# Dense MoE on one core: the first product by one level of Strassen's scheme, with its row operands kept in DRAM

## The chip, the core and the metric

One core of a Trainium2 chip. The metric is the device time of one execution in microseconds (us). The engines are named as in the profile: PE (TensorE, matmuls), PEld (its weight loads), DVE (VectorE), ACT (ScalarE), POOL (GpSimd), SP (SyncE, which issues most of the DMAs). Everything is float32; each matmul operand is split into a high and a low part, and each product is made of three matmuls, high·high, high·low and low·high.

## The reference

Three stages, each the input of the next (N = 2304 rows, D = 512, E = 8 experts, F = 1024):

```
# 1. attention with a threshold, 4 batches x 8 heads x 576 x 64
scores = scale * q @ k.T
scores = where(scores >= max(scores) - tau, scores, -1e9)
attn_out = softmax(scores) @ v            # -> x (2304, 512)

# 2. dense MoE: every row goes through every expert
P = exp(x @ w_gate - max)                 # then 8 rounds of row and column normalisation
for e in range(E):
    h = np.maximum(x @ w1[e], 0.0)        # (2304,512) @ (512,1024)
    out += P[:, e:e+1] * (h @ w2[e])      # (2304,1024) @ (1024,512)

# 3. top-1 MoE: each row goes through one expert, scaled by its gate
idx = argmax(x @ w_gate2); out[row] = gate * (relu(x[row] @ v1[idx]) @ v2[idx])
```

## The kernel before, in words

`attention` leaves x transposed (512 features on 4 x 128 partitions, 2304 rows along the free side) in the tile `xall`. `moe1` is the dense stage, `moe2` the top-1 stage. No queue is written by hand. Every piece of work is handed to a list planner (`Sched`) as `op(name, engine, cost, due time, function, what it depends on, acq, rel)`; `acq` and `rel` take and return counted resources such as PSUM banks ("h", "y") or buffers. The planner fills one list per engine, which is the order in which that engine then issues. An engine's list is strict: an instruction that waits holds up all behind it.

`moe1` before walks 8 experts; in each, 6 chunks of 384 rows; in each, 8 blocks of 128 columns of F. One block is

- `g1` (L567): 12 matmuls of 384 columns, x·w1 into one of 4 "h" banks,
- `relu_hi` on ACT (L572) and `relu_lo` on DVE (L576): the split of max(h, 0), 128x384,
- `g2` (L583): 3 row tiles x 3 matmuls of 512 columns into the chunk's 3 "y" banks.

At the end of a chunk DVE adds Pm[:, e] * y to the row sums `acc` (L691, `y_acc`), 128x512 each. Weights arrive by `ld_w` (L528, L530), are split by ACT (`rnd`, L539) and POOL (`w_lo`, L551). The rows of a chunk are split anew for each expert: `x_hi` on ACT (L539), `x_lo` on POOL (L560). `gate` (L598) forms the logits of the dense stage.

Before, `moe2` starts while the last expert of `moe1` runs: when a row tile's sum is final it is transposed (`tx1`, L872), split by ACT and DVE (`ev1` L881, `ev1l` L884), multiplied with the second gate (`lg1` L890, `lg3` L900), ranked, and stored. A table of row numbers then says which rows go to which expert. Row tiles below `TE` count into an early table, the others into a late one. Slots of gathered rows run through L1239 (first product, `hp`) and L1258 (second, `py`); their weights are loaded at L1195 and split at L1223 (ACT) and L1227 (DVE); the gathered rows are transposed at L1208 (`tx`) and split at L1216 and L1219.

Of the kernel before, what the change touches and what calls it, by code (L numbers as in the profile page):

```python
# [116 lines left out]
def attention(tc, sc, cst, dram, xT, q, k, v, tau, also=None):  # L117
# [11 lines left out]
    with ExitStack() as ctx:  # L129
# [296 lines left out]
        for p in range(NP):  # L426
# [70 lines left out]
            for half in range(2):  # L497
# [13 lines left out]

def moe1(tc, sc, cst, pools, xT, acc, wgs, w1, w2, NE=8, NW=9):
    nc = tc.nc
    E, Dm, FF = w1.shape
    N = xT[0].shape[1]
    CH = 384
    NCH, NF, NK, NT = N // CH, FF // 128, Dm // 128, N // 128
    one, wp, stg, xs_p, h_p, bank = pools
# [14 lines left out]
    WH = lambda e, f: V if e == 0 and f == 2 else A
    WL = lambda e, f: V if e == 0 and f != 2 else G
    XH = lambda e, c: A

    def rnd(eng, out, in_):
        if eng == A:
            nc.scalar.copy(out, in_)  # L539
        elif eng == V:  # L540
            nc.vector.tensor_copy(out, in_)
        else:
            nc.gpsimd.tensor_scalar(out, in_, 1.0, 1.0, op0=ALU.mult, op1=ALU.mult)

    def w_hi(e, f):
        wt[e, f] = wp.take()
        rnd(WH(e, f), wt[e, f][:, 0], wr[e, f])

    def w_lo(e, f):
        t = wt[e, f]  # L550
        (nc.vector if WL(e, f) == V else nc.gpsimd).tensor_tensor(t[:, 1], wr[e, f], t[:, 0].bitcast(F32), op=ALU.subtract)  # L551
# [936 lines left out]
```

## Time and profile before

| what | us |
|---|---|
| median of 3 runs (2291.84 to 2294.73) | 2293.86 |
| the profiled execution | 2292.15 |
| its span, first to last instruction | 2290.4 |
| attention | 0 to 338 |
| dense stage (`moe1`), its first and last `g1` | 342.9 to 1972.7 |
| top-1 stage, its main part | 1987 to 2235 |
| tail (last products, evictions, stores) | 2235 to 2290.4 |

The profile's page gives busy times over the whole span; a stage's limit is read from the windows (busy time of each engine in a stretch) and from the chain of waits (which work each step waited for, followed back from the last instruction). In the groups of instructions, "idle before" is the time in which the engine had nothing to do just ahead of such an instruction, and the releaser is what ended it.

### The profile page before, as it was taken

Reading aid. Unit: us, or ns where it says so; the run is one execution under the profiler, and the core shown is the slowest. Engines: PE = TensorE matmul, PEld = TensorE weight load, DVE = VectorE, ACT = ScalarE, POOL = GpSimd, SP = SyncE. Lnnn points to the kernel's source line nnn. Section 1 sums busy time; section 2 is a strip of 40 time slices with the busy share of each in tenths; the row PEclk is TensorE's granted clock in tenths of the full one; section 3 lists DMA queues with packets and bytes.
Section 4 is the critical chain, followed back from the end, with each engine's and each line's share of the span. In section 5 each row is a group of like instructions: output and inputs, shape, how many; then the busy total and the mean of one; then the engine's idle time right before and its main releaser. Section 6 shows DMA issues by size and latency. Waiting matters only on the chain.

```text
span 2290.4 us, 31977 instructions
## 1 busy us (share of the span) xinstructions
PE 2254.2 (98%) x12699; PEld 2048.7 (89%) x12699; DVE 887.6 (39%) x1904; ACT 780.0 (34%) x1394; POOL 634.5 (28%) x641
## 2 busy tenths in 40 slices
PE   7999999999999999999999999999999999999997
PEld 7999988888899999999999999999999888888886
DVE  8999973113412212211211212112112243775673
ACT  6888862113112211311221131122113121455673
POOL 6777762104302301410230141123014010021220
PEclk9999999999999999999999999999999999999999
DMA  3222112002000100200010020001001011568860
GB/s 95 64 59 63 43 44 83 1 1 74 1 1 19 56 1 1 74 1 1 19 56 1 1 74 1 1 19 56 1 1 37 14 28 33 218 226 298 277 213 13
DMA packets 101691, 129.66 MB, mean 57 GB/s; under 512 B 19006, under 2 KB 64206, under 8 KB 101520
## 3 DMA queue, kind: packets, MB, share of 16 engines
q1 hardware_dynamic: 97696, 118.10, 16.1%
q0 software_dynamic: 3840, 9.45, 1.1%
q8 instruction: 102, 1.67, 0.3%
q14 instruction: 53, 0.43, 0.1%
HBM read 118.52 MB, written 13.18 MB: 58 GB/s over the span
## 4 chain that ended last, share of the span: by engine, by line
PE 93%; issue 2%; DVE 2%; DMA 2%; ACT 1%; SPq 0%; POOL 0%; POOLq 0%; ACTq 0%; DVEq 0%
PE h L567 35%; PE y L583 35%; PE pt_av L407 4%; PE s L282 4%; PE py L1258 4%; PE hp L1239 4%; PE pt_m L350 2%; PE sh L1270 1%; PE pt_k L251 1%; PE sy L1300 1%; PE pt_av L410 1%; DMA out_dram<-ys,idi 0%; PE pt_q L241 0%; PE tx L1208 0%; PE lt L598 0%
## 5 line engine op out<-in xcount | busy, mean ns | idle before, releaser
L567 PE MATMUL h<-xs,w 128*128 128x384 f32 x4608 | 871.0, 337 | 1.6 <-ACT w L539 1.0
L583 PE MATMUL y<-w,hh 128*128 128x512 f32 x3456 | 867.0, 394 | 0.6 <-DVE hh L576 0.6
L567 PEld LDWEIGHTS h<-xs,w 128*128 128x128 f32 x4608 | 819.0, 188 | 35.7 <-ACT w L539 1.4
L583 PEld LDWEIGHTS y<-w,hh 128*128 128x128 f32 x3456 | 640.2, 188 | 117.9 <-DVE hh L576 1.0
L576 DVE SCALAR_TENSOR_TENSOR hh<-h,hh 128x384 fp32r<-128x384 f32 x384 | 214.1, 558 | 1210.4 <-ACT hh L572 1210.3
L572 ACT ACTIVATE hh<-h 128x384 fp32r<-128x384 f32 x384 | 188.9, 492 | 1173.5 <-PE h L567 1150.7
L560 POOL TENSOR_TENSOR xs<-xall,xs 128x384 fp32r<-128x384 f32 x192 | 189.1, 1017 | 1114.6 <-ACT xs L539 1114.6
L551 POOL TENSOR_TENSOR w<-wr,w 128x1024 fp32r<-128x1024 f32 x57 | 137.0, 2404 | 116.6 <-ACT w L539 112.3
L407 PE MATMUL pt_av<-PTh,vsp 128*128 128x288 f32 x512 | 144.4, 323 | 0.0
L1239 PE MATMUL hp<-xst,w 128*128 128x256 f32 x960 | 121.6, 284 | 0.2 <-DVE xst L1219 0.2
L1239 PEld LDWEIGHTS hp<-xst,w 128*128 128x128 f32 x960 | 117.7, 191 | 2.6 <-DVE xst L1219 1.6
L304 ACT ACTIVATE p<-s,stat 128x576 f32<-128x576 f32 x144 | 108.2, 753 | 29.8 <-DVE stat L287 29.5
L310 DVE SCALAR_TENSOR_TENSOR p<-s,stat,p 128x576 f32<-128x576 f32 x144 | 116.0, 808 | 5.0 <-ACT p L304 2.2
L1258 PE MATMUL py<-w,hp 128*128 128x512 f32 x480 | 113.1, 393 | 1.6 <-ACT hp L1246 0.9
L287 DVE TENSOR_REDUCE stat<-s 128x1 f32<-128x576 f32 x144 | 108.1, 752 | 12.7 <-PE s L282 12.4
L1258 PEld LDWEIGHTS py<-w,hp 128*128 128x128 f32 x480 | 88.9, 188 | 20.2 <-ACT hp L1246 1.2
L282 PE MATMUL s<-kk,qst 128*128 128x288 f32 x512 | 96.0, 310 | 2.5 <-DVE p L310 2.2
L539 ACT CAST w<-wr 128x1024 fp32r<-128x1024 f32 x63 | 66.1, 1049 | 92.1 <-PE y L583 85.6
L407 PEld LDWEIGHTS pt_av<-PTh,vsp 128*128 128x128 f32 x512 | 91.8, 188 | 1.5
L691 DVE SCALAR_TENSOR_TENSOR acc<-y,Pm,acc 128x512 f32<-128x512 f32 x126 | 86.5, 743 | 0.8 <-POOL acc L687 0.8
L539 ACT CAST xs<-xall 128x384 fp32r<-128x384 f32 x192 | 84.7, 511 | 0.0
L366 POOL TENSOR_TENSOR PTl<-rp,PTh 128x512 fp32r<-128x512 f32 x64 | 82.5, 1289 | 4.3
(237 smaller groups left out, 1780.3 us busy)
## 6 DMA issues: line engine op xcount, KB each, us to landing
wr<-in_moe_w_dram SPq DMA_DIRECT2D x128, 256.0 KB, 3.1
xall<-in_moe_w_dram SPq DMA_DIRECT2D x56, 512.0 KB, 5.3
acc<-in_moe_w_dram SPq DMA_DIRECT2D x56, 512.0 KB, 3.8
kr<-in_k_dram SPq DMA_DIRECT2D x16, 256.0 KB, 2.8
qr<-in_q_dram SPq DMA_DIRECT2D x16, 256.0 KB, 3.0
vr<-in_v_dram SPq DMA_DIRECT2D x16, 256.0 KB, 2.8
rbc<-rd SPq DMA_DIRECT2D x32, 128.0 KB, 3.0
x1d<-acc SPq DMA_DIRECT2D x28, 128.0 KB, 2.4
```

The lines of the kernel that those rows point to most:

```text
L282: nc.tensor.matmul(ps[:, half, 0:288], lh, kk[p][:, h, s, half * 288:(half + 1) * 288], start=(i == 0 and s == 0), stop=(i == len(parts) - ...
L310: nc.vector.scalar_tensor_tensor(t, stile.pop(g)[:, :, 0:288], s[:, 1, j:j + 1], t, op0=ALU.is_ge, op1=ALU.mult, accum_out=s[:, 2, j:j + 1])
L407: nc.tensor.matmul(ps[:, 0:288], vv[:, h * 4 + kc, i, 64 - 64 * h:192 - 64 * h], mv[:, h, kc, c0:c1], start=(h == 0 and kc == 0 and n == 0 ...
L539: nc.scalar.copy(out, in_)
L551: (nc.vector if WL(e, f) == V else nc.gpsimd).tensor_tensor(t[:, 1], wr[e, f], t[:, 0].bitcast(F32), op=ALU.subtract)
L560: nc.gpsimd.tensor_tensor(t[:, 1, k], xT[k][:, c * CH:(c + 1) * CH], t[:, 0, k].bitcast(F32), op=ALU.subtract)
L567: nc.tensor.matmul(ps[:, 0:CH], w[:, i, k * 128:(k + 1) * 128], x[:, j, k], start=(k == 0 and i + j == 0), stop=(k == NK - 1 and i == 1))
L572: nc.scalar.activation(hh[e, c, f][:, 0], hps[e, c, f][:, 0:CH], AF.Relu)
L576: nc.vector.scalar_tensor_tensor(t[:, 1], hps.pop((e, c, f))[:, 0:CH], 0.0, t[:, 0].bitcast(F32), op0=ALU.max, op1=ALU.subtract)
L583: nc.tensor.matmul(yps[e, c, t], h[:, i, t * 128:(t + 1) * 128], w[:, j, 512:1024], start=(f == 0 and i + j == 0), stop=(f == NF - 1 and i ...
L1239: nc.tensor.matmul(ps[:, r * 256:(r + 1) * 256], w[:, i, f * 128:(f + 1) * 128], x[:, j, k * 256:(k + 1) * 256], start=(k + r + i + j == 0 ...
L1258: nc.tensor.matmul(T["y", s, h], t[:, i, c:c + 128], w[:, j, r * 512:(r + 1) * 512], start=(b + r + i + j == 0), stop=(b == 3 and r == 1 a ...
```

## The change

It replaces `moe1`'s first product, keeps the second, and moves the memory around them.

- **Products.** Rows go in 3 chunks of 768, each as two halves of 384; F in 32 panels of 256 (4 for each expert), each as two halves of 128; D as two halves of 256. One panel and one chunk were 8 half products (two halves each of rows, F and D); now 7 are made (`PROD`, `g1`, L630), 6 matmuls of 384 columns each, of sums of the quarters: `m0` and `m1` into one bank, `m2` into a second, `m3` and `m5` into one, `m4` and `m6` into one. `m1` is added into the bank of `m0` once ACT has copied `m0` out (`ev_s`, L635). DVE then makes the quarters from the banks with five sums of 128x384 (`u2`, `u3`, `c22`, `c21`, `c12`, all L638) into an SBUF ring. Four `rhi` (ACT, L660) and four `rlo` (DVE, L665) split the quarters; `g2` (L679) makes 12 x 3 matmuls of 512 columns as before. "h" has 2 banks, "y" 6.
- **Order of visits.** `visits()`: an expert is two groups of two panels, each group goes over the 3 chunks; the last expert is a group of one panel (chunks 2, 1, 0) and a group of three (chunks 0, 1, 2). There are 48 visits; y leaves PSUM 6 times per visit (L778, L780, L782).
- **Row operands.** `xs[m]`, m = 0..6, 128 x 2 x 768 each (786 KB), are built in the first group only: differences T1 to T4 on POOL (L533, L568), `xhi` on ACT (L608), `xlo` on DVE or POOL (L568). Each is stored to DRAM (`xst`, L614) and loaded again for every later visit (`xld`, L617) whose chunk differs from that of the visit before, when the last panel of that visit has run its product m.
- **Weights.** A panel loads 512 KB of w1 (`ld1`, L574) and 512 KB of w2 (`ld2`, L578); POOL makes four sums of 128 x 2 x 128 (`wsteps`), ACT and DVE split seven operands and w2.
- **Memory.** The row sums live in `xall`, whose rows are no longer needed after the first group. `moe2`'s buffers are rings of pieces that `moe1` gives back. `x1t` is now one buffer instead of two, `TE` is 12 instead of 14.
- **Gate.** The logits are built from four of the operands, in 60 matmuls of 384 columns instead of 48.

The diff, cut to its core:

```diff
-        for k in range(NK):
-            for i, j in ((0, 0), (0, 1), (1, 0)):
-                nc.tensor.matmul(ps[:, 0:CH], w[:, i, k * 128:(k + 1) * 128], x[:, j, k],
-                                 start=(k == 0 and i + j == 0), stop=(k == NK - 1 and i == 1))
+CH, HC = 768, 384
+PROD = ((0, None), (1, 0), (5, None), (4, None), (2, None), (3, 3), (6, 4))
+    for nm, n in (("h", 2), ("y", 6), ("as", 3), ("w2", 3), ("r1", 1), ("r2", 1), ("it", 5), ("hq", 6)):
+        sc.res(nm, n)
+    def xst(c, m):
+        nc.sync.dma_start(out=xd[c, m], in_=xs[m].bitcast(F32))
+    def xld(c, m):
+        nc.sync.dma_start(out=xs[m].bitcast(F32), in_=xd[c, m])
+    def g1(v, p, m):
+        a, on = PROD[m]
+        if on is None:
+            hb[v, p, m] = bank(f"h{v}_{p}_{m}")
+        ps = hb[v, p, m if on is None else on]
+        w = AS[p % 3]
+        for k in range(2):
+            for i, j in SPL:
+                nc.tensor.matmul(ps[:, 0:HC], w[:, i, a, k * 128:(k + 1) * 128], xs[m][:, j, k * HC:(k + 1) * HC],
+                                 start=(on is None and k + i + j == 0), stop=(k == 1 and i == 1), skip_group_check=True)
+    def ev_s(v, p):
+        it[v, p, "u"] = itr.take()
+        nc.scalar.copy(it[v, p, "u"], hb[v, p, 0][:, 0:HC])
+    def add(out, ps, x):
+        nc.vector.tensor_tensor(out, ps[:, 0:HC], x, op=ALU.add)
...
+                op(("xld", v, m), Y, .6, u, partial(xld, c, m), free + [("xso", c, m)] + [("gl", NCH - 1, h) for h in range(2)])
...
+                dep += {1: [("ev_s", v, p)], 5: [("u3", v, p)], 6: [("c22", v, p)]}.get(m, [])
...
-TE = 14
+TE = 12
...
-            T["x", i // TG] = wp.take()
+            T["x", i // TG] = x1t
```

How the order moves, at three places. PE in the middle of `moe1`, before (h_<chunk>_<block> is a block's first product, y_<chunk>_<tile> the second):

```order
L567 MATMUL h_1_6_9761<-xs_1_9416,w_5061 128x384 x12
L583 MATMUL y_1_0_9644<-w_5060,hh_1_5_9752 128x512 x3
L583 MATMUL y_1_1_9652<-w_5060,hh_1_5_9752 128x512 x3
L583 MATMUL y_1_2_9656<-w_5060,hh_1_5_9752 128x512 x3
L567 MATMUL h_1_7_9786<-xs_1_9416,w_5062 128x384 x12
```

and after, one panel (h_<panel>_<product whose bank it is>; the second h_15_0 is m1, the second h_15_3 is m5, the second h_15_4 is m6):

```order
L630 MATMUL h_15_0_10173<-xa,as_5057 128x384 x6
L679 MATMUL y_5_10180<-w_2_5063,hq 128x512 x3
L630 MATMUL h_15_0_10173<-xa,as_5057 128x384 x6
L679 MATMUL y_0_10130<-w_2_5063,hq 128x512 x3
L679 MATMUL y_1_10143<-w_2_5063,hq 128x512 x3
L630 MATMUL h_15_2_10201<-xb,as_5057 128x384 x6
L679 MATMUL y_2_10149<-w_2_5063,hq 128x512 x3
L679 MATMUL y_3_10162<-w_2_5063,hq 128x512 x3
L630 MATMUL h_15_3_10216<-xb,as_5057 128x384 x6
L679 MATMUL y_4_10167<-w_2_5063,hq 128x512 x3
L679 MATMUL y_5_10180<-w_2_5063,hq 128x512 x3
L630 MATMUL h_15_4_10231<-xb,as_5057 128x384 x6
```

Instead of 12 and 9 in turn, six matmuls of a product alternate with one or two tiles of the second product of the panel before. Between m0 and m1 stands a single tile (y_5, 3 matmuls).

PE in the last expert, where the finished row tiles enter the top-1 stage, before:

```order
L872 MATMUL x1t_14973<-ident,acc_5067 128x128 x4
L872 MATMUL x1t_14978<-ident,acc_5067 128x128 x4
L567 MATMUL h_1_2_14984<-xs_1_14727,w_5062 128x384 x12
L890 MATMUL l1t_15000<-w_5059,wg_73 16x256 x8
L583 MATMUL y_1_0_14954<-w_5061,hh_1_1_14958 128x512 x3
L900 MATMUL lg_15016<-ident,lts 128x16 x2
```

and after:

```order
L630 MATMUL h_29_3_15399<-xb,as_5060 128x384 x6
L679 MATMUL y_4_15139<-w_1_5062,hq 128x512 x3
L679 MATMUL y_5_15156<-w_1_5062,hq 128x512 x3
L1050 MATMUL x1t_15419<-ident,xall 128x128 x4
L679 MATMUL y_0_15425<-w_2_5063,hq 128x512 x3
L679 MATMUL y_1_15433<-w_2_5063,hq 128x512 x3
L1050 MATMUL x1t_15439<-ident,xall 128x128 x4
L679 MATMUL y_2_15444<-w_2_5063,hq 128x512 x3
L1068 MATMUL l1t_15450<-x_5066,wg_73 16x256 x8
L1080 MATMUL lg_15460<-ident,lts 128x16 x2
L1050 MATMUL x1t_15466<-ident,xall 128x128 x4
L1050 MATMUL x1t_15479<-ident,xall 128x128 x4
...
L630 MATMUL h_29_4_15534<-xb,as_5060 128x384 x6
```

Where the transposes and logits of two tiles stood among products, those of six tiles (three pairs) now stand in a row ahead of m4; the second and third pair (seven rows; two of them shown) have no product between them. This happens twice, in the last two visits.

SP in `moe1`, before (two weight loads for each block):

```order
L528 DMA wr_7_5227<-in_moe_w_dram 128x4x128
L530 DMA wr_7_5227<-in_moe_w_dram 128x512
L528 DMA wr_0_5252<-in_moe_w_dram 128x4x128
L530 DMA wr_0_5252<-in_moe_w_dram 128x512
```

and after:

```order
L617 DMA xa<-xops 128x1536 x2
L617 DMA xb<-xops 128x1536 x5
L617 DMA xa<-xops 128x1536
L574 DMA fw<-in_moe_w_dram 128x4x256
L617 DMA xa<-xops 128x1536
L617 DMA xb<-xops 128x1536 x4
L578 DMA fw<-in_moe_w_dram 128x2x512
```

Weight loads now stand among the reloads of the seven operands, in one queue.

## Rows read from the trace of the kernel before

**Rows 1.** The page: span and the busy time of each engine (share of the span, instructions).

```profile
span 2290.4 us, 31977 instructions
PE 2254.2 (98%) x12699; PEld 2048.7 (89%) x12699; DVE 887.6 (39%) x1904; ACT 780.0 (34%) x1394; POOL 634.5 (28%) x641
```

**Rows 2.** The windows: from and to, us; PE, PEld, DVE, ACT and POOL busy (instructions), granted TensorE clock as a share of full speed, DMA share, GB/s.

```profile
800.00:1800.00 1000.00, 1000.00 (x5017) 906.06 (x5016) 192.44 (x329) 207.63 (x398) 209.61 (x157) 1.00 0.06 20
1800.00:1950.00 150.00, 150.00 (x805) 133.28 (x804) 56.35 (x221) 30.61 (x69) 14.71 (x17) 1.00 0.14 32
2055.00:2075.00 20.00, 18.37 (x121) 16.95 (x122) 9.27 (x9) 9.40 (x12) 4.36 (x4) 1.00 1.04 398
2100.00:2230.00 130.00, 130.00 (x759) 114.28 (x759) 90.77 (x93) 88.22 (x111) 27.73 (x23) 1.00 0.75 246
```

**Rows 3.** The chain of waits, a stretch in the middle of the dense stage: start us, length us, what.

```profile
605.94 2.10 PE h L567 x12
608.04 2.08 PE y L583 x9
```

**Rows 4.** The timeline of the same stretch: start us, length us, engine, line, operation, tiles, forms, count, idle time before and its releaser.

```profile
605.55 2.17 PEld L567 LDWEIGHTS h<-xs,w 128*128 128x128 f32 x12
605.78 2.27 PE L567 MATMUL h<-xs,w 128*128 128x384 f32 x12
607.88 2.24 PE L583 MATMUL y<-w,hh 128*128 128x512 f32 x9
608.08 0.50 ACT L572 ACTIVATE hh<-h 128x384 fp32r<-128x384 f32 x1 [5.02 <-PE h L567]
608.61 0.56 DVE L576 SCALAR_TENSOR_TENSOR hh<-h,hh 128x384 fp32r<-128x384 f32 x1 [4.96 <-ACT hh L572]
```

**Rows 5.** The page's groups of instructions of the dense stage: busy us, mean ns of one, idle us before and what ended most of it.

```profile
L567 PE MATMUL h<-xs,w 128*128 128x384 f32 x4608 | 871.0, 337 | 1.6 <-ACT w L539 1.0
L583 PE MATMUL y<-w,hh 128*128 128x512 f32 x3456 | 867.0, 394 | 0.6 <-DVE hh L576 0.6
L576 DVE SCALAR_TENSOR_TENSOR hh<-h,hh 128x384 fp32r<-128x384 f32 x384 | 214.1, 558 | 1210.4 <-ACT hh L572 1210.3
L572 ACT ACTIVATE hh<-h 128x384 fp32r<-128x384 f32 x384 | 188.9, 492 | 1173.5 <-PE h L567 1150.7
L539 ACT CAST w<-wr 128x1024 fp32r<-128x1024 f32 x63 | 66.1, 1049 | 92.1 <-PE y L583 85.6
L691 DVE SCALAR_TENSOR_TENSOR acc<-y,Pm,acc 128x512 f32<-128x512 f32 x126 | 86.5, 743 | 0.8 <-POOL acc L687 0.8
```

**Rows 6.** The timeline where PE is released by another engine (1985 to 1987 us).

```profile
1985.58 1.28 DVE L1219 TENSOR_TENSOR xst<-tx,xst 128x512 fp32r<-128x512 f32 x2
1986.91 1.34 PE L1239 MATMUL hp<-xst,w 128*128 128x256 f32 x9 [0.24 <-DVE xst L1219]
```

**Rows 7.** The timeline where row tiles enter the top-1 stage (1839 to 1846 us).

```profile
1839.04 1.91 PE L872 MATMUL x1t<-ident,acc 128*128 128x128 f32 x16
1843.57 1.08 PE L890 MATMUL l1t<-w,wg 128*16 128x256 f32 x8
1844.68 0.36 ACT L895 COPY lts<-l1t 16x256 f32<-16x256 f32 x1 [0.42 <-PE l1t L890]
1846.76 0.17 DVE L904 COPY lgs<-lg 128x16 f32<-128x16 f32 x1
```

**Rows 8.** The groups again, of the splits of 512 columns in the top-1 stage, and of the gate's first matmuls.

```profile
L884 DVE TENSOR_TENSOR w<-x1t,w 128x512 fp32r<-128x512 f32 x18 | 11.5, 686 | 10.8 <-ACT w L881 10.8
L881 ACT CAST w<-x1t 128x512 fp32r<-128x512 f32 x18 | 9.5, 589 | 10.1 <-PE x1t L872 10.1
L598 PE MATMUL lt<-xs,wg 128*16 128x384 f32 x48 | 9.3, 336 | 1.4 <-issue 1.4
```

**Rows 9.** The chain of waits at the seam of attention and dense stage.

```profile
337.65 1.44 issue
339.08 1.40 PE lt L598 x7
340.50 1.05 ACT w L539
341.58 1.24 DVE w L551
342.86 3.27 PE h L567 x17
```

**Rows 10.** The chain of waits from the dense stage's last product on, and where the late table's first rows arrive.

```profile
1972.70 0.50 ACT hh L572
1973.56 6.67 DMA xall<-in_moe_w_dram
1986.91 2.30 PE hp L1239 x17
...
2049.04 7.46 DMA xall<-x1d,idi
2056.63 0.63 PE tx L1208 x4
```

**Rows 11.** The page's DMA issues: size of each, median us from issue to landing.

```profile
xall<-in_moe_w_dram SPq DMA_DIRECT2D x56, 512.0 KB, 5.3
```

More of the change, by code (lines that the diff above doesn't have):

```diff
@@ L510, in attention, with x_diff, visits, moe1 @@
         sc.run()
-def moe1(tc, sc, cst, pools, xT, acc, wgs, w1, w2, NE=8, NW=9):
+CH, HC = 768, 384
+SPL = ((0, 0), (0, 1), (1, 0))
+PROD = ((0, None), (1, 0), (5, None), (4, None), (2, None), (3, 3), (6, 4))
+QUART = ((0, 0), (1, 1), (1, 0), (0, 1))
+UN = 3.75
+def x_diff(nc, xall, c):
+    r = xall[:, c * 4 * CH:c * 4 * CH + 2 * CH].rearrange("p (k h n) -> p h k n", k=2, h=2)
+    nc.gpsimd.tensor_tensor(r[:, 1], r[:, 1], r[:, 0], op=ALU.subtract)
+def visits(NE=8, NCH=3):
+    V, g = [], 0
+    for e in range(NE):
+        last = e == NE - 1
+        for n, ps in enumerate(((0,), (1, 2, 3)) if last else ((0, 1), (2, 3))):
+            for c in (range(NCH - 1, -1, -1) if last and n == 0 else range(NCH)):
+                V.append((e, g, c, [4 * e + p for p in ps]))
+            g += 1
+    return V
+def moe1(tc, sc, cst, pools, xall, acc, wgs, w1, w2, xd, give):
     nc = tc.nc
     E, Dm, FF = w1.shape
[L515 to L518, printed above, removed]
+    N = xall.shape[1] // 4
+    NCH, NT = N // CH, N // 128
+    one, fw, AS, W2, xs, hq, bank = pools
     ident, ones = cst["ident"], cst["ones"]
@@ L533, in moe1 @@
[L533 to L551, printed above, removed]
@@ new lines, in g2 @@
+    def g2(v, p, q, n):
+        f, h = QUART[q]
+        t = 3 * h + n
+        ps_ = vis[v][3]
+        first = p == ps_[0] and q < 2
+        if first:
+            yps[v, t] = bank(f"y{v}_{t}")
+        x, w = hh[v, p, q], W2[p % 3]
+        for i, j in SPL:
+            nc.tensor.matmul(yps[v, t], x[:, i, n * 128:(n + 1) * 128], w[:, j, f * 512:(f + 1) * 512],
+                             start=(first and i + j == 0), stop=(p == ps_[-1] and q > 1 and i == 1))
+        if n == 2:
+            hring.give(hh.pop((v, p, q)))
@@ L829, in moe2 @@
     NT = N // 128
-    one, wp, stg, xs_p, h_p, bank = pools
+    one, fw, x1t, rings, bank = pools
+    wp, xs_p, h_p, stg, rawr = (rings[n] for n in ("w", "xs", "hh", "wr", "raw"))
     ident, ones = cst["ident"], cst["ones"]
@@ L1214, in txh @@
         if h == 0:
[L1215 removed]
+            T["xs", s] = (h_p if single(s) else xs_p).take()
         nc.scalar.copy(xv(s, h, 0), T["tx", s, h].rearrange("p (k c) -> p k c", k=4))
@@ L1242, in q1 @@
             wp.give(T.pop(("w", s, k)))
+            if k == 3:
+                xs_p.give(T.pop(("xs", s)))
     def prh(s, b):
-        T["hh", s, b] = h_p.tile([128, 2, 512], F32R, name=f"hp{s}_{b}", tag="hh")
+        T["hh", s, b] = h_p.take()
         nc.scalar.activation(T["hh", s, b][:, 0], T["hp", s, b], AF.Relu)
@@ L1452, in attention_moe_moe2_kernel @@
     sc.alias = {"h": "b8", "y": "b8", "b": "b8"}
-    moe1(tc, sc, cst, pools, xT, acc, mt["wg"][0], w1, w2)
-    rest = moe2(tc, sc, cst, mt, pools, xall, accs, acc, w12, w22, out, w1.shape[0] - 1)
+    wdone = moe1(tc, sc, cst, (mem, fw, AS, W2, xs, hq, bank), xall, acc, mt["wg"][0], w1, w2, xd, give)
+    vis = visits(w1.shape[0])
+    ulast = sum(len(x[3]) for x in vis if x[1] < vis[-1][1])
+    rest = moe2(tc, sc, cst, mt, (mem, fw, x1t, rings, bank), xall, acc, w12, w22, out, ulast, vis[-1][1], wdone)
     sc.run()
```

454 lines of the change are left out of this document (303 added, 151 removed).

## The prediction

> **What bounds the kernel now.** I read the page's engine line first: PE is busy in 98% of the span, no other engine in more than 39% [rows 1]. That is a mean over stages, so the windows come next. From 800 to 1800 us PE is busy in 1000.00 of 1000.00 us, and from 1800 to 1950 in 150.00 of 150.00, at a granted clock of 1.00, while ACT and DVE are busy about a fifth of the first stretch [rows 2]. The chain of waits says the same: 12 first-product matmuls in 2.10 us, 9 second-product ones in 2.08, and so on, with no piece of another engine between [rows 3]. The dense stage is thus a stream of matmuls; what it costs is the number of matmuls times their spacing, and everything else matters only if it makes PE wait. The spacings: 2.10/12 = .175 us for 384 columns, 2.08/9 = .231 us for 512 (the group's means of 337 and 394 ns [rows 5] overlap each other and are not spacings).
>
> **The term that is removed.** The first product has 4608 matmuls [rows 5]; seven of eight are 4032. The new ones have the same 384 columns and weights of the same size, so 576 x .175 = **100.8 us** less. The second product stays: 96 panel-chunks (32 panels x 3 chunks) x 36 = 3456 matmuls of 512 columns, the number of before. A rule speaks for a smaller gain here: the Trainium skill, TensorE: Matmul & The Clock Gate, section "Back-to-back issue gap", gives an isolated gap of columns/2.4 GHz plus 2.5 ns. That would be .1625 us for 384 columns, and 93.6 us for the term. By the row's .175 it is 100.8, and I use the row.
>
> **One panel, walked.** A product of six matmuls takes h = 1.05 us, a tile of the second product .69. From a panel's start: m0 to 1.05, one tile to 1.75, m1 to 2.80, two tiles, m2 to 5.24, two tiles, m3 to 7.68, two tiles, m4 to 10.12, one tile, m5 to 11.87, two tiles, m6 to 14.31, two tiles, end at 15.70. What each wait needs:
>
> - *m1 waits for ACT's copy of m0.* Where a product ends and the next begins at 607.88, ACT starts .20 later [rows 4]; such an ACT piece takes .49 [rows 5]; PE restarts .05 after its releaser (DVE ends at 1986.86, matmul at 1986.91) [rows 6]. Together .74, against a cover of one tile, .69: lost at least .05. If the weight load, which usually runs .23 ahead of its matmul (605.55 and 605.78) [rows 4], must wait too, up to .27. I take .12, nearer the lower end since in rows 6 load and matmul start together. 96 x .12 = **+11.5** (5 to 26).
> - *m2 to m6* wait for DVE's sums. One is about .56, as L576 with the same tiles [rows 5]. u2 ends about 6.0, its bank is wanted at 9.07; u3 at 8.4 for 10.8; c22 at 10.9 for 13.3; c21 at 12.6 for 15.7. Two us or more of slack: nothing, as long as DVE's list is not held. A panel gives DVE 9 pieces of .56, 5.0 us; in the worst panel six evictions of .74 [rows 5] and the weight splits of one panel (two of .69, one of about 1.0, one of 1.3, from the .69 of 512 columns [rows 8] by columns) come to it, 13.2 of 15.7. If that cover goes, every late sum shows on PE directly (rival B).
> - *Weight casts* on ACT stand ahead of a copy in some 32 panels. A cast of 512 is .59 and of 1024 1.05 [rows 5, 8]; most lie in ACT's gaps; I take .08 each, **+2.5** (0 to 10).
>
> **Reloads.** A visit of two panels (31.4 us) loads 7 x 786 KB = 5.5 MB, and on average .67 MB of weights, 197 GB/s. Operand m is free when the last panel of a visit has run product m, and wanted 14.6 us later; the seven pass SP's queue between 1.05 into that panel and 13.3 into the next, 28 us, which asks 197 GB/s without and 221 with weights. The top-1 stage moves 398 GB/s from 2055 to 2075, and 246 over 130 us in which PE never stops (130.00 of 130.00) [rows 2]; a 512 KB load lands 5.3 us after issue [rows 11]. So nothing is lost, and PE is not slowed. In SP's list weight loads stand ahead of some reloads; at a change of group they hold it for about 6 us, which the 14.6 cover.
>
> **Smaller terms.** The gate: 48 matmuls of 384 columns become 60, 12 x .175 = **+2.1** [rows 8]. Seam to attention: before, PE idles between 337.65 and 342.86 except for the 1.40 of gate matmuls, 3.8 us [rows 9]; now nothing can fill the wait for operand and weight, about 5.3: **+2** (0 to 6); T1 on POOL beside attention's end **+1**. The first three visits build operands on ACT, DVE and POOL while PE runs: **+3** (0 to 10). The seam to the top-1 stage, where PE still waits for DVE and a load [rows 10], with buffers that now come back piece by piece: **+2.5** (-3 to 8).
>
> **Row tiles entering the top-1 stage.** Before, such transposes stand among products and PE loses nothing [rows 2, 7]. In the new order three pairs stand in a row ahead of m4, with one free "h" bank. For the second and third pair I chain: four transposes .44 (1.91/16 x 4), +.20, ACT .59, +.03, DVE .69, +.05 [rows 4, 6, 7, 8], twice; logits .91; ACT's copy .20 + .36 + .05; their transposes .22; DVE's two of .17 and hops .6 [rows 7]. That is 6.3 us with 2.0 of PE work, 4.3 lost. The first pair has three tiles between: 1 to 2 lost. About 9.5 for a cluster, two clusters: **+19** (8 to 28).
>
> **The late table.** Its rows arrive 83.9 us after the last dense product (1972.70 to 2056.63) [rows 10], on a chain of DVE pieces and loads. With TE = 12 one pair more is ranked late: two DVE splits of .69 and some 26 pieces of .17 = 5.8, **+6** (0 to 12).
>
> **Sum.** -100.8 + 11.5 + 2.5 + 2.1 + 2 + 1 + 3 + 2.5 + 19 + 6 = -51.2. Against the profiled execution's 2292.15 (span 2290.4 [rows 1], 1.75 around it; 1.7 below the median of 2293.86) that is **2241 us**. A measurement of this kernel tells about 0.2% (4.6 us) from no change.
>
> **Rivals.**
>
> *A. Nearly the whole product comes through.* ACT's copy hides but for .05 a panel (5 us), the clusters cost 8, the late table and the seams are absorbed (4), gate 2. For it: PE's waits in the dense stage of before come to 2.2 us in all [rows 5]. Against it: the new order has a one-tile cover that is arithmetically too short. 2292 - 100.8 + 19 = about 2210.
>
> *B. The in-order chains hold PE oftener.* ACT and DVE carry about twice the pieces per panel; when an eviction or weight split stands ahead of a sum, the wait reaches PE. For it: two "h" banks instead of four, and the two-step chain ACT then DVE for every quarter. Against it: two us of slack on each. With .35 us more on each of 96 panels, +34: about 2275.
>
> *C. Slower: SP's queue does not keep up.* The mechanism is one: reloads of a visit run at less than PE asks, and PE waits at m0..m6 of every visit with a new chunk (43). For the forecast it decides below about 197 GB/s without weights, 221 with them; the whole gain of 51 is gone when each of 43 visits loses 1.2 us, so when 5.5 MB take 29.2 us (188 GB/s; with weights in the same stretch 211). At 180 GB/s without weights a visit takes 30.6, loses 2.6, 43 x 2.6 = 112, and the time is 2241 + 112, about 2350. For it: the dense stage of before moves only 20 GB/s [rows 2], so this load beside full PE is new, and each load of 512 KB takes 5.3 us to land [rows 11]: one at a time, 512/5.3 is 99 GB/s. Against it: 246 GB/s beside PE at 130.00 of 130.00, and 398 [rows 2], which only loads that overlap can give. The Trainium skill, DMA: Bandwidth & Descriptors, section "Anatomy of one DMA", fits one DMA as 2.0 us plus bytes at 436 GB/s, an estimate of 3.8 us for 786 KB; seven in a row, without overlap, would be 26.6 of the 28 us, and two weight loads among them would make PE wait. The trace's 398 GB/s speaks against loads that run alone.
>
> *D. No gain from fewer matmuls.* If the weight loads set the pace, spacings could grow: PEld is busy 906 of 1000 us [rows 2]. But a load goes with each matmul, so they fall alike, and the pieces alternate more finely. About 2290.
>
> **Chances.** The forecast (2220 to 2262) .60, A .12, B .19, C .06, D .03. The range reaches from A to B: **2207 to 2277**; it leaves out C, D and the ends of A and B. Faster .91, same .03, slower .06.
>
> **What would show it.** In the windows, the dense stage's share of PE busy below 1.00, by .12 of 15.8 us a panel; in the waits, "h" for ACT's copy (L635), 96 times, as the greatest; a first product with 4032 matmuls; first to last dense product 1540 to 1600 us instead of 1630; DMA at about 200 GB/s in it and no wait of PE for a reload (L617); two gaps of about 9 us in the last expert at L1050; the late rows some 6 us later after the last dense product. Wrong would be: waits for L617, waits for L638 beyond a few us, or spacing of 384 columns other than .175.

## The result, and the profile after

| | before | after |
|---|---|---|
| median, us | 2294.16 | 2239.26 (2238.26 to 2241.91) |
| ratio, 95% interval | | 0.9764 (0.9747 to 0.9781) |
| span of the profiled execution | 2290.4 | 2237.6 |

The changed kernel is 54.9 us faster between medians and 52.8 in the profiled spans; 2241 was forecast. Here is the page of the changed kernel, first its engines, then groups of instructions of the dense stage (they answer to [rows 1, 5]):

```profile
span 2237.6 us, 32615 instructions
PE 2183.4 (98%) x12133; PEld 1949.6 (87%) x12133; DVE 1379.4 (62%) x2678; ACT 797.0 (36%) x1384; POOL 464.0 (21%) x541
...
L679 PE MATMUL y<-w,hq 128*128 128x512 f32 x3456 | 913.1, 395 | 2.7 <-DVE hq L665 1.7
L630 PE MATMUL h<-xb,as 128*128 128x384 f32 x2880 | 580.5, 336 | 0.3 <-DVE fw L638 0.3
L638 DVE TENSOR_TENSOR fw<-h,fw 128x384 f32<-128x384 f32 x480 | 267.3, 557 | 299.8 <-PE h L630 297.7
L630 PE MATMUL h<-xa,as 128*128 128x384 f32 x1152 | 241.4, 344 | 8.5 <-ACT as L581 5.0
```

The first product has 2880 + 1152 = 4032 matmuls; a DVE sum takes the .56 that was assumed, and PE waited for such sums for .3 us in the whole run. DVE's share went from 39% to 62%, and in the middle of the dense stage that cost nothing that shows. The bound engine got less work, an idle one more.

The windows (columns as in [rows 2]):

```profile
350.00:372.00 22.00, 12.93 (x39) 10.07 (x39) 18.43 (x12) 9.26 (x13) 21.50 (x12) 0.61 0.84 310
1000.00:1200.00 200.00, 200.00 (x989) 177.77 (x988) 103.33 (x167) 43.44 (x80) 13.57 (x16) 1.00 0.58 204
1032.00:1040.00 8.00, 8.00 (x42) 7.17 (x41) 4.90 (x7) 2.61 (x4) 3.83 (x4) 1.00 1.01 375
1800.00:1850.00 50.00, 46.14 (x247) 38.00 (x246) 29.46 (x116) 10.90 (x24) 0.00 (x0) 1.00 0.27 79
```

The middle moves 204 GB/s, in bursts of 375, beside a PE that is busy throughout. The start (350 to 372) is full of POOL, has a TensorE clock of .61 and leaves PE idle for 9 us; the last expert (1800 to 1850) leaves it idle for 3.9.

The chain of waits through one panel (start us, length us, what; 599.65 is m1, 608.89 m5, 614.82 the tile between m0 and m1, 615.52 the next m1):

```profile
599.65 1.24 PE h L630 x6
600.89 1.39 PE y L679 x6
602.28 1.04 PE h L630 x6
...
608.19 0.70 PE y L679 x3
608.89 1.06 PE h L630 x6
...
614.82 0.70 PE y L679 x3
615.52 1.24 PE h L630 x6
```

and the timeline of its hand-off from m0 to m1:

```profile
598.79 0.86 PE L679 MATMUL y<-w,hq 128*128 128x512 f32 x3
599.04 0.48 ACT L635 COPY fw<-h 128x384 f32<-128x384 f32 x1 [1.31 <-PE h L630]
599.58 1.00 PEld L630 LDWEIGHTS h<-xa,as 128*128 128x128 f32 x6 [0.37 <-ACT fw L635]
```

The chain is PE alone, as in [rows 3], but m1 takes 1.24 where the others take 1.04. The weight load starts .06 after ACT is done (599.04 + .48 = 599.52), after .37 of idle time: it waits too, the case that the prediction priced at up to .27. "Busy" hides this: the window says 200.00 of 200.00, and in the timeline the record of the three matmuls ahead of m1 runs from 598.79 to 599.65, up to where m1 begins in the chain. The prediction looked for the loss in the share of PE busy and in waits for L635; neither shows it, the chain does.

**Where the time went, by stretch.** The second product has the same 3456 matmuls in both kernels, 36 for a panel and chunk, so the starts of its n-th matmul cut the two traces at the same work:

| stretch | before, us | after, us | difference | of it first product | of it work moved over a cut | rest | rest as forecast |
|---|---|---|---|---|---|---|---|
| 0 to the end of attention's last product | 337.6 | 348.4 | +10.7 | 0 | 0 | +10.7 | +1 |
| to the 433rd matmul (12 panels) | 220.0 | 227.9 | +8.0 | -11.6 | +4.2 | +15.4 | +8.9 |
| to the 3025th (72 panels) | 1210.0 | 1138.1 | -71.9 | -75.6 | -4.2 | +7.9 | +10.5 |
| to the 3456th (12 panels) | 214.6 | 210.7 | -3.9 | -13.6 | -2.4 | +12.1 | +20.8 |
| to the end | 308.2 | 312.5 | +4.3 | 0 | +2.4 | +1.9 | +8.5 |

(A panel here is one panel with one chunk; its product is 1.05 us. The forecast's 14 us for hand-off and casts are spread over the 96 panels.) The matmuls of the first product are counted in each stretch: 66, 432 and 78 fewer, at .175. Two other pieces of work lie on different sides of a cut in the two kernels. The 19 matmuls of the row and column normalisation come after the 433rd before (two panels took 18.8 us there instead of 16.75, 4.2 more in all), and ahead of it now. And with `TE` = 12 one pair of row tiles less enters the top-1 stage ahead of the 3456th (six pairs instead of seven, some 2.4 us for a pair in the panels of the kernel before). Both prices are estimates from the kernel before, and the same price is taken for the changed one.

The rests are against the kernel before, so what that one lost in the same stretch is taken off. They sum to 48.0; 49.6 was forecast (the last column is rounded). So the total came out right, but the parts did not: attention and the start cost 16 more than forecast, the middle, the clusters (the rows of waits in the last two visits) and the end 18 less. The experiments go through them.

### The profile page after: what moved, and what is told of

It is laid out like the page before. It is cut to its first block, busy times and chain, and to the rows that moved or that the text cites. A ratio compares the mean times of both kernels' runs of the same rounds, so it can differ in the third digit from the quotient of the medians.

```text
span 2237.6 us, 32615 instructions
## 1 busy us (share of the span) xinstructions
PE 2183.4 (98%) x12133; PEld 1949.6 (87%) x12133; DVE 1379.4 (62%) x2678; ACT 797.0 (36%) x1384; POOL 464.0 (21%) x541
## 4 chain that ended last, share of the span: by engine, by line
PE 87%; issue 5%; DMA 3%; DVE 2%; ACT 1%; POOL 1%; SPq 0%; POOLq 0%; ACTq 0%; DVEq 0%
PE y L679 35%; PE h L630 32%; PE pt_av L407 4%; PE s L282 4%; PE hp L1425 3%; PE py L1446 2%; PE pt_m L350 2%; DMA out_dram<-fw,idi 2%; PE pt_k L251 1%; PE pt_av L410 1%; DMA xall<-in_moe_w_dram 1%; DMA fw<-x1d,idi 1%; PE lt L695 0%; PE pt_q L241 0%; PE l1t L1068 0%
## 5 line engine op out<-in xcount | busy, mean ns | idle before, releaser
L679 PE MATMUL y<-w,hq 128*128 128x512 f32 x3456 | 913.1, 395 | 2.7 <-DVE hq L665 1.7
L679 PEld LDWEIGHTS y<-w,hq 128*128 128x128 f32 x3456 | 638.2, 188 | 97.2 <-DVE hq L665 3.1
L630 PE MATMUL h<-xb,as 128*128 128x384 f32 x2880 | 580.5, 336 | 0.3 <-DVE fw L638 0.3
L630 PEld LDWEIGHTS h<-xb,as 128*128 128x128 f32 x2880 | 515.9, 188 | 42.5 <-DVE fw L638 0.6
L638 DVE TENSOR_TENSOR fw<-h,fw 128x384 f32<-128x384 f32 x480 | 267.3, 557 | 299.8 <-PE h L630 297.7
L660 ACT ACTIVATE hq<-fw 128x384 fp32r<-128x384 f32 x288 | 151.2, 525 | 764.9 <-DVE fw L638 759.3
L568 POOL TENSOR_TENSOR fw<-fw 128x256 f32<-128x256 f32 x96 | 83.0, 865 | 1115.0 <-DMA fw<-in_moe_w_dram 976.4
L665 DVE SCALAR_TENSOR_TENSOR hq<-fw,hq 128x384 fp32r<-128x384 f32 x288 | 167.6, 583 | 139.4 <-ACT hq L660 137.6
L630 PE MATMUL h<-xa,as 128*128 128x384 f32 x1152 | 241.4, 344 | 8.5 <-ACT as L581 5.0
L630 PEld LDWEIGHTS h<-xa,as 128*128 128x128 f32 x1152 | 202.6, 189 | 43.5 <-ACT fw L635 23.5
L782 DVE SCALAR_TENSOR_TENSOR xall<-y,Pm,xall 128x512 f32<-128x512 f32 x252 | 181.1, 748 | 14.5 <-PE y L679 2.8
L665 DVE SCALAR_TENSOR_TENSOR hq<-h,hq 128x384 fp32r<-128x384 f32 x96 | 53.4, 557 | 216.4 <-ACT hq L660 216.4
L660 ACT ACTIVATE hq<-h 128x384 fp32r<-128x384 f32 x96 | 47.2, 492 | 145.9 <-PE h L630 145.9
L568 DVE TENSOR_TENSOR as<-fw,as 128x512 fp32r<-128x512 f32 (+1 forms) x96 | 76.0, 817 | 9.4 <-ACT as L581 9.3
```

The source lines that it names most:

```text
L568: sub = lambda e, out, x, y: e.tensor_tensor(out, x, y, op=ALU.subtract)
L630: nc.tensor.matmul(ps[:, 0:HC], w[:, i, a, k * 128:(k + 1) * 128], xs[m][:, j, k * HC:(k + 1) * HC], start=(on is None and k + i + j == 0) ...
L638: nc.vector.tensor_tensor(out, ps[:, 0:HC], x, op=ALU.add)
L660: nc.scalar.activation(hh[v, p, q][:, 0], it[v, p, q] if q else hb[v, p, 0][:, 0:HC], AF.Relu)
L665: nc.vector.scalar_tensor_tensor(t[:, 1], x, 0.0, t[:, 0].bitcast(F32), op0=ALU.max, op1=ALU.subtract)
L679: nc.tensor.matmul(yps[v, t], x[:, i, n * 128:(n + 1) * 128], w[:, j, f * 512:(f + 1) * 512], start=(first and i + j == 0), stop=(p == ps_ ...
```

## The experiments

Ratios below are against the kernel before; differences against the changed kernel's 2239.3. Beside these runs the kernel before had medians from 2291.98 to 2293.76, so a difference of one or two us tells nothing by itself; the n-th matmuls of the traces tell more.

**The product's price.** m2 twice:

```diff
-        for k in range(2):
+        for r in range(2 if m == 2 else 1):
+            for k in range(2):
...
```

> The product m2 is made twice in every panel (576 more matmuls of 384 columns, the output is not the reference's, all else stays). Theory: an added product costs what the removed one gave, 96 x 1.05 = 101 us; total 2340, so the surroundings of the seven products (hand-offs, start, attention, seams) cost 46 us over the kernel before. Rival: in the new order the matmul stream has holes in which a product is nearly free, or the spacing has changed: total below 2325 or above 2355.

Measured 2342.26, +103.0. From the 865th to the 3025th matmul of the second product (60 panels) a panel takes 16.85 us instead of 15.81: 1.04 for a product, 99.8 in 96 panels. (The second pass starts the bank anew, so the output stays that of the changed kernel, other than expected.) The stream has no holes in which a product is free, and what surrounds the seven products costs 48 us.

**The hand-off.**

```diff
-            op(("ev_s", v, p), A, .49, U(0), partial(ev_s, v, p), [("g1", v, p, 0)], acq=["it"])
+            op(("ev_s", v, p), A, .8, U(0), partial(ev_s, v, p), [("g1", v, p, 0)], acq=["it"])
```

> One number: the planner is told .8 instead of .49 for ACT's copy of m0, so that it puts two tiles of the second product between m0 and m1 in every panel. Theory: m1's wait for that copy costs .18 to .20 us in the two thirds of the panels that have one tile there (64 of 96), 12 to 13 us in all; then a panel takes 15.6 to 15.7 us throughout and the total falls to about 2227. Rival: the loss moves on to m2, which now has a single tile ahead of it, or to a sum of DVE; then panels stay at 15.8 or more and the total at 2236 to 2241.

Measured 2230.48 (ratio 0.9731, 0.9715 to 0.9748), -8.8, some 3 us short of the theory. A panel takes 15.69 us instead of 15.81; over 96 panels that is 11.5, and the trace is 10.4 ahead after 90 panels, of which 1 comes from attention; the two clusters give 1.3 back. The loss did not move on to m2. It was there in two panels of three: in the others the planner had put two tiles between m0 and m1 by itself.

**T1 in attention.**

```diff
-        for c in range(2):
-            ...
-            op(("T1", c), G, 2., 9. * (4 * bs[-1] + 4), partial(x_diff, nc, xall, c), [...])
...
-                t = {0: ("T1", 2., lambda c=c: x_diff(nc, xall, c), []) if c == 2 else None,
+                t = {0: ("T1", 2., lambda c=c: x_diff(nc, xall, c), []),
```

> T1 of chunks 0 and 1 is taken out of attention's planner and made in the dense stage, as chunk 2's always was; nothing else changes. Theory: T1's two POOL pieces in attention's plan moved attention's order, and its last product ended 10.7 us later (348.4 us instead of 337.7); then attention ends at 337 to 339 us again, the dense stage's start grows by one POOL piece of 1.8 to 2.8 us, and the total falls by 7 to 10 us against the changed kernel (2239), to about 2230. Rival: attention grew because of the split eviction of its last tile or the row layout, which stay; then it still ends near 348 and the total stays within 3 us of 2239.

Measured 2238.89, -0.4. The chain of waits of this run at attention's end and where the dense stage runs full:

```profile
337.87 0.16 DVE xall L419
...
338.45 0.47 DVE xall L419
...
361.96 6.72 PE h L627 x28
```

and of the changed kernel:

```profile
347.87 0.50 PE pt_av L410 x2
...
348.39 0.47 DVE xall L419
349.00 1.56 ACT xa L608 x2
...
353.87 2.22 POOL xb L568
...
357.49 2.52 POOL xall L568
...
368.55 2.85 DVE w L568
...
372.58 2.37 PE h L630 x12
```

The theory's mechanism held: without the two POOL pieces in its plan attention ends 10.8 us sooner (337.6), and all its 2576 matmuls stand in the order of the kernel before, where in the changed kernel 1041 stand elsewhere. Its sum did not hold: from attention's end to the 37th matmul of the second product it takes 44.1 us instead of 39.5. One of the two pieces ran ahead of attention's end (at 333.0), the other now stands among the first visit's pieces on POOL (at 358.3). Of 9.5 us at the first tile 5.2 are left after three panels, 2.7 and 1.5 after the two clusters; those last losses I have not explained.

**The start: who holds whom.** First, T2 to T4 and three low parts of the first chunk from POOL to DVE:

```diff
-                     2: ("T2", 2., lambda c=c: sub(nc.gpsimd, X, R(c, 1, 1), R(c, 0, 1)), [...]),
+                     2: ("T2", 2., lambda c=c, w=(nc.vector if c == 0 else nc.gpsimd): sub(w, X, R(c, 1, 1), R(c, 0, 1)), [...]),
...
-                en = V if m < 4 else G
+                en = V if m < 4 or c == 0 else G
```

> For the first chunk alone T2, T3, T4 and the low parts of operands 4 to 6 are made by DVE instead of POOL (T1 stays in attention). Theory: between 349 and 372 us POOL and DVE hold each other up (DVE's pieces of two SBUF tensors take 2 to 2.9 us there instead of 1.0 to 1.2, POOL's 2.2 to 2.8 instead of 1.8), so what counts is the sum of both; six POOL pieces of 1.8 become six DVE pieces of about 1, the first 36 matmuls of the second product come 4 to 6 us sooner, total 2233 to 2236. Rival: the two only run beside each other slowly for other reasons (DMA traffic), then DVE, which is already busy in all of it, gets longer by 6 us and the total rises to 2242 to 2245.

Measured 2246.13, +6.9: 1 us beyond the rival's range, and not for the rival's reason. DVE in the changed kernel, POOL being busy all the while:

```profile
354.35 3.96 DVE L568 TENSOR_TENSOR xa<-xall,xa 128x768 fp32r<-128x768 f32 x2
358.22 2.86 DVE L568 TENSOR_TENSOR w<-fw,w 128x1024 fp32r<-128x1024 f32 x1
```

and in this run, POOL idle until 363.7, then at work again:

```profile
359.92 0.94 DVE L568 TENSOR_TENSOR xb<-xall,xb 128x768 fp32r<-128x768 f32 x1
360.79 0.95 DVE L568 TENSOR_TENSOR xall<-fw,xall 128x768 f32<-128x768 f32 x1
...
365.40 2.58 DVE L568 TENSOR_TENSOR xb<-xall,xb 128x768 fp32r<-128x768 f32 x1
```

A piece of 768 columns takes .95 us alone and 1.98 (mean of two) or 2.58 beside POOL; 1024 columns take 1.21 and 2.86. The .95 were measured at the granted clock of .50 and at 392 GB/s (360 to 365 us), so neither is the reason. But six pieces more in DVE's one list stand ahead of what the second product waits for, and the first 36 matmuls of it come 3.4 us later instead of sooner.

Then the same six pieces by ACT, as plain copies (this leaves out the differences and the low parts, so the values are wrong):

```diff
-                     2: ("T2", 2., lambda c=c: sub(nc.gpsimd, X, R(c, 1, 1), R(c, 0, 1)), [...]),
+                     2: ("T2", 2., lambda c=c: sub(nc.gpsimd, X, R(c, 1, 1), R(c, 0, 1)) if c else nc.scalar.copy(X, R(c, 1, 1)), [...]),
...
+                if c == 0 and m > 3:
+                    op(("xl", c, m), A, .85, u, lambda m=m, s=src(c)[m]: nc.scalar.copy(k2(xs[m][:, 1]), s), [("xh", c, m)])
```

> In the first chunk T2, T3, T4 and the low parts of operands 4 to 6 are made by ACT as plain copies (their values are wrong, so the output is not the reference's), POOL keeps only the weight sums. Theory: the dense stage's start is long because POOL's and DVE's pieces of two SBUF tensors exclude each other; with six POOL pieces gone DVE's pieces of 768 columns take .95 us instead of 2 and of 1024 columns 1.2 instead of 2.9, DVE is done 7 to 9 us sooner and the full rate comes at 364 to 367 us instead of 372.6. Rival: DVE's long pieces come from the DMA traffic or from the lower clock of that stretch; they stay at 2 to 2.9 us and full rate comes later than 370.

Its two executions took 5489.02 and 2235.91 us, and the profile is of the first, in which attention alone ends at 789.7 us, so the start can't be read from it. Hence once more:

> The kernel of e10_act once more, whose profiled execution ran at less than half the speed in every stage, attention too, and can't be read (T2 to T4 and the low parts of operands 4 to 6 of the first chunk by ACT as plain copies, values wrong; POOL keeps the weight sums). Theory, narrowed by the run with those pieces on DVE, where DVE's pieces of 768 columns took .95 us as long as POOL was idle, at the same clock and DMA rate: with six POOL pieces gone DVE is done sooner, and the first 36 matmuls of the second product are reached 4 to 8 us before the changed kernel's 387.8; total 2231 to 2236. Rival: the weight sums on POOL and the order of the chain set the start, not the six pieces: less than 2 us sooner.

Measured 2235.9, -3.4. The first 36 matmuls come 5.3 us sooner, 1.0 of which is attention, which ended sooner in this run; after two panels it is 3.9. DVE:

```profile
356.61 1.21 DVE L568 TENSOR_TENSOR w<-fw,w 128x1024 fp32r<-128x1024 f32 x1
357.74 0.95 DVE L568 TENSOR_TENSOR as<-fw,as 128x768 fp32r<-128x768 f32 x1
358.61 0.95 DVE L568 TENSOR_TENSOR xb<-fw,xb 128x768 fp32r<-128x768 f32 x1
```

So the six POOL pieces and the hold-up that they bring cost some 3 to 4 us. The start lost 13.1: from attention's last product to the 37th matmul of the second product it takes 39.5 us instead of 26.4, for the same matmuls (72 of the first product, 8 of the gate, 36). The rest is, by the chain of waits, the serial way from attention's last tile and the weights' arrival over sums, splits and the first products, where the kernel before had only splits ([rows 9]); no run took that apart.

**Weights earlier.**

```diff
-    fw = tile_("fw", [5760], F32)
+    parts = ((0, tile_("f0", [1024], F32)), (3072, tile_("f2", [2688], F32)), (1024, tile_("f1", [2048], F32)))
...
```

> The staging memory is cut into three tiles, so that the first weight loads need not wait for the end of all of attention's memory: they can be issued after attention's last SP transfer (343.6 us) instead of at 349.0. Theory: the weight sums on POOL and splits on ACT and DVE of the first panel then lie in attention's end; the first product starts some 4 us sooner and full rate comes 5 to 8 us sooner, total 2231 to 2235. Rival: the start is bound by the row operands, which need attention's last tile; then the total stays within 2 us of 2239.

Measured 2242.51 (2240.95 to 2244.54), +3.2; its interval of the ratio (0.9766 to 0.9799) overlaps the changed kernel's. The edit did not do what it was for: the first load was still issued at 348.90 (348.98 in the changed kernel), and the first 36 matmuls came at the same time. What an earlier load would give was not tried.

**The clusters.**

```diff
-        u = cend(TG * c + TG - 1) + 0.1
+        u = cend(TG * c + TG - 1) + 0.1 + (.5 * (c % 3) if TG * c < TE else 0)
```

> Only the due times of the three pairs of row tiles of one chunk move apart (by half a planner unit each), so that m4, m5 and m6 and tiles of the second product stand between the pairs' transposes and logits. Theory: in the changed kernel the two clusters take 28.5 and 29.3 us where a panel takes 15.8, with 5.8 us of work of their own, so 7 to 8 us each are waits for the ACT and DVE chains; with work between them the two stretches shrink by 4 to 7 us each and the total falls by 6 to 12, to 2227 to 2233. Rival: ACT's and DVE's lists are the limit there, so that the products merely wait in other places; the two stretches stay within 2 us and so does the total.

Measured 2230.0 (ratio 0.9728, 0.9712 to 0.9745), -9.3. The two stretches took 23.3 and 23.3 us instead of 28.5 and 29.2, and the panel behind each some 1 us more than in the changed kernel.

**The reloads.** Each made twice, into the same place:

```diff
+        for r in range(2):
+            nc.sync.dma_start(out=xs[m].bitcast(F32), in_=xd[c, m])
...
```

> Every reload of a row operand is made twice, 11 MB for each visit with a new chunk instead of 5.5, with the same data. Theory (the reload has room): loads overlap and move up to some 400 GB/s; 11 MB in the 28 us of a visit asks 393 GB/s and with weights more than that, so PE waits 0 to 4 us in each of 43 visits: 2240 to 2410, and DMA shares of .9 to 1.0 in the dense stage. Rival (the reload is already near its limit at 200 GB/s): a visit then takes 1.5 to 2 times its 31.5 us, total above 2900.

Measured 3087.2, the rival's time, and still no answer on the rival. The waits of SP's queue in this run (us, times, longest):

```profile
SPq L618 <- DMA xb<-xops: 1146.3, 215, 6.5
SPq L618 <- DMA xa<-xops: 406.1, 86, 6.7
```

The second transfer, which writes the same tile, waits for the first to land, 1552/301 = 5.2 us each, and holds the queue. The experiment made loads one at a time; it shows only what that would cost. With the extra bytes going elsewhere:

```diff
...
+        turn = nld[0] = nld[0] + 1
         nc.sync.dma_start(out=xs[m].bitcast(F32), in_=xd[c, m])
+        nc.sync.dma_start(out=extra[turn % 21], in_=xd[c, m])
...
```

> Beside each reload of an operand one more transfer of the same 786 KB from DRAM to DRAM, to its own place, which nothing waits for. Twice the bytes pass the queue, 11 MB for a visit with a new chunk, without the wait that held the doubled reload. Theory (room is left): the queue moves 375 GB/s and more, so that a visit of 31.6 us keeps its pace or waits up to 4 us: 2240 to 2410. Rival (the reload is near its limit at 200 GB/s): reloads come late by 10 us and more in each of 43 visits, total above 2650.

Measured 2317.7, +78.4. Its windows and PE's waits:

```profile
1000.00:1400.00 400.00, 387.18 (x1882) 340.02 (x1881) 200.16 (x321) 82.59 (x152) 27.94 (x32) 0.99 0.87 353
...
1030.00:1040.00 10.00, 10.00 (x50) 8.89 (x49) 3.34 (x6) 1.29 (x3) 0.00 (x0) 1.00 1.09 452
```

```profile
PE h L634 <- DMA xb<-xops: 41.3, 30, 2.9
```

At twice the bytes the queue keeps up 353 GB/s and 452 in bursts, and PE begins to wait: 78.4/43 is 1.8 us for each visit with a reload. The change asks 204, so as an estimate from this one mix, about half of it copies from DRAM to DRAM, it has room for some 353/204 = 1.7 times its traffic.

**Together.** First all five edits (T1 of the first chunk on DVE):

> All together: T1 out of attention (the first chunk's on DVE), two tiles ahead of m1, clusters pulled apart, the first chunk's operands on DVE, weights earlier. Theory: attention ends at 338 (10 us), the start gains 8 to 14, the hand-off 9, the clusters 6 to 12, less some overlap: 2239 less 30 to 40, 2199 to 2209. Rival: gains at the start are given back at the clusters or the table, as with T1 alone: above 2220.

Measured 2221.97 (ratio 0.9691, 0.9675 to 0.9707), -17.3: the rival's time, 13 us short of the theory. Hand-off and clusters add up, but after two panels the trace is only 1.5 us ahead, where T1 alone was 6.2 ahead: DVE's longer list, as in the run with those pieces on DVE. So without the pieces on DVE, and with T1 held back to where POOL idles:

```diff
-            op(("T1", c), G, 2., 9. * (4 * bs[-1] + 4), ..., [("x", 4 * b + hp, half) for ...])
+            op(("T1", c), G, 2., 9. * (4 * bs[-1] + 4), ..., [("x", 4 * b + hp, half) for ...] + [("x", 14, 1)])
...
-            op(("ev_s", v, p), A, .49, ...
+            op(("ev_s", v, p), A, .8, ...
...
-        u = cend(TG * c + TG - 1) + 0.1
+        u = cend(TG * c + TG - 1) + 0.1 + (.5 * (c % 3) if TG * c < TE else 0)
```

> Two tiles ahead of m1 and the clusters pulled apart, as in the two runs before, and T1 of chunks 0 and 1 held back until attention's last pair but one is evicted, so that POOL makes them in its idle time at attention's end. Theory: attention's order stays that of the kernel before and ends at 338 to 340 us; the hand-off gives 9, the clusters 9, attention and start together 5 to 9 us, all in places that don't meet: 2239 less 23 to 27, 2212 to 2216. Rival: the two T1 pieces now stand at the dense stage's start and cost it what attention gains, as T1 in the dense stage did: 2219 to 2222.

Measured **2216.69** (ratio 0.9662, 0.9649 to 0.9675), 22.6 faster than the changed kernel and 77 than the kernel before, just above the range of the theory. Attention ends at 339.35, with 22 of its matmuls in another place than before. By the second product's matmuls it is 8.4 ahead after 12 panels (attention and start), 17.0 after 84 (hand-off), 28.2 after the last (clusters); 5.6 of these are given back in the top-1 stage.

## Why the prediction was right, and where it was right by luck

- **The removed products**: right in size (100.8; 99.8 by the doubled product). The spacing in the new order is 1.04/6 = .173, the row's .175. The isolated gap of the Trainium skill, TensorE: Matmul & The Clock Gate, section "Back-to-back issue gap", .1625, would have made it 93.6, as an estimate; both traces decide for the row.
- **Hand-off m0 to m1**: right mechanism, and the total is right because two sizes were off against each other: .18 to .20 instead of .12 where it happens (the weight load waits too), but in 64 of 96 panels. That is 11.5 to 12.8, against 11.5.
- **Casts on ACT**: 2.5 was forecast. The middle's rest is 7.9, and the hand-off's 72 x .12 = 8.6 alone is more than that, so no cost of casts can be seen.
- **Attention and seam**: the step that failed. "T1 on POOL beside attention's end +1" took the pieces' time beside other work and overlooked that a list planner makes another order when two pieces are added: attention ended 10.7 us later. The three runs without T1 in the middle of attention's plan show it (it ends at 337.6, 338.3 and 339.4 there). That the order did it, and not the 3.7 us of POOL that the two pieces take, is not shown separately; in the last run the pieces run in attention (at 326.9 and 328.7), the order is nearly that of before, and attention ends 1.7 us later than before. And the start, forecast at 2 + 3, cost 13.1, all of it ahead of the 37th matmul of the second product: the walk of panel 0 counted waits one by one at the durations of undisturbed rows, but there POOL and DVE hold each other up, and every split has a sum ahead of it. The second and third visit, which also build operands, cost nothing that shows.
- **Clusters**: too dear at 19. The two panels take 28.5 and 29.2 us, 26.1 more than two plain ones of 15.81, and the work of their three pairs is some 5.8 each, so 14.5 are lost (an estimate; in the second cluster the granted clock was .50 for 3.4 us, from 1878.3). The stretch's rest is less, 12.1, as it is against a kernel that spent 2.4 us on a pair, too. The chain took one free bank; the transposes of two tiles run back to back in two (eight in 1.09 us), so a pair comes after 5.0 us, not 6.3, with 3.0 lost, not 4.3:

```profile
1813.49 1.09 PE L1050 MATMUL x1t<-ident,xall 128*128 128x128 f32 x8
1815.41 0.64 PE L1068 MATMUL l1t<-x,wg 128*16 128x256 f32 x4 [0.83 <-ACT x L1059]
1817.12 0.64 PE L1068 MATMUL l1t<-x,wg 128*16 128x256 f32 x4 [1.06 <-DVE x L1062]
...
1818.48 1.09 PE L1050 MATMUL x1t<-ident,xall 128*128 128x128 f32 x8
```

- **Late table and last seam**: 8.5 were forecast, 1.9 are left in the table. [Rows 10] were read as if the last dense product ended at 1972.70; the trace of the kernel before has twelve more matmuls of L567 until 1977.28, so its late rows come after 79.4 us, not 83.9. In the changed kernel they come after 89.7, 10 us more where 6 were forecast. But PE had other products to run meanwhile, and waited for them no longer than before, 1.60 us instead of 1.93. What failed is the assumption that later rows hold PE. The last products and the late rows, first before, then after:

```profile
1975.01 2.27 PE L567 MATMUL h<-xs,w 128*128 128x384 f32 x12
2056.63 0.63 PE L1208 MATMUL tx<-ident,xall 128*128 128x128 f32 x4 [1.93 <-DMA xall<-x1d,idi]
...
1917.18 1.31 PE L630 MATMUL h<-xb,as 128*128 128x384 f32 x6
2008.18 0.66 PE L1395 MATMUL tx<-ident,fw 128*128 128x128 f32 x4 [1.60 <-DMA fw<-x1d,idi]
```

- **Rivals.** A (2210) was not met, but the three edits of the last run come within 7 us of it. B is refuted: PE waited .3 us for DVE's sums. C is refuted: among PE's waits from 350 to 1925 us there is none for a DMA, at bursts of 375 GB/s; the run with twice the bytes shows the room. The estimate of 3.8 us for one load was low, though (its section is on DMAs that GpSimd issues, these are issued by SP): the medians are 4.2 and 6.1 us, and PE does not wait because the loads overlap; the run with loads one at a time shows what they cost otherwise. D is refuted by the price of the doubled product.

So 2241 against 2239.3 is in part luck: the price of the products and the sum for the hand-off were right; among the rest, misses of +16 and -18 us cancelled.

## What to carry to other kernels

When an engine is busy in 98%, count its instructions and use the spacing from the chain, not the mean duration of a record; that term was right to 1%. Cut two traces at the same work (the n-th instruction of a kind that both have) before explaining a total, and count what else lies on each side of the cut: here errors of +16 and -18 had cancelled. And when a planner makes the order, no added piece is free because its engine has idle time: look at whether the order around it stays.

## What was not expected of the hardware

- DVE's pieces with two inputs in SBUF took 1.98 to 2.86 us beside POOL's pieces, .95 to 1.21 alone, and POOL's of 768 columns took 2.5 instead of 1.8. The Trainium skill, SBUF — State Buffer, section "Who interferes with whom", says that such a DVE instruction contends with a GpSimd instruction that reads SBUF; the page's section "Summary: rules for kernel authors" says that the second to issue blocks until the first is done. The trace agrees: DVE's pieces grow by 1.0 to 1.65 us, up to nearly one piece of POOL, and POOL's by .7, less than one piece of DVE. POOL, with DVE idle and with DVE at work:

```profile
349.06 1.81 POOL L568 TENSOR_TENSOR fw<-xall 128x768 f32<-128x768 f32 x1 [5.90 <-DVE xall L419]
...
361.63 2.53 POOL L568 TENSOR_TENSOR xall<-xall,fw 128x768 f32<-128x768 f32 x1
```

- The granted clock fell to .50 (1.2 GHz) while PE idled from 348.4 to 353.3, and was back at 1.00 just before 370, with PE busy in 4.76 of the 5 us up to there. Before, PE idled in the same place for less (1.44 us, then two waits of under 1 us) and the clock stayed at 1.00. By their record six matmuls of 384 columns took 2.29 us there, and 1.21 to 1.34 at full clock. PE was mostly waiting in that stretch, so what the clock itself cost there was not measured. The windows (columns as in [rows 2]), then PE:

```profile
350.00:355.00 5.00, 0.69 (x1) 0.29 (x1) 1.63 (x2) 4.33 (x6) 4.50 (x4) 0.76 0.80 290
360.00:365.00 5.00, 3.00 (x8) 1.77 (x6) 5.00 (x4) 2.01 (x3) 5.00 (x4) 0.50 0.99 333
365.00:370.00 5.00, 4.76 (x13) 4.08 (x14) 4.91 (x4) 1.92 (x3) 5.00 (x3) 0.54 0.99 391
```

```profile
353.34 0.69 PE L630 MATMUL h<-xa,as 128*128 128x384 f32 x1 [4.99 <-ACT as L581]
359.49 2.29 PE L630 MATMUL h<-xa,as 128*128 128x384 f32 x6 [0.57 <-ACT fw L635]
```

- A 786 KB reload took 4.2 or 6.1 us to land (the medians of its two tiles), and transfers beside a PE that was busy in the whole window reached 375 GB/s, and 452 with copies from DRAM to DRAM among them.
